# Attention followed by an expert layer on one core: biases from constants in two parts, v cast in halves, q on GpSimd, a mask bank taken at first need

## The chip, the cores and the metric

The kernel runs on one core of one Trainium2 chip. The metric is the device time of one execution in microseconds (us); lower is better. The *span*, from the first to the last instruction of the core in the profile's records, is given beside it. In each comparison the kernels ran on the same chip, interleaved with the kernel before. An execution is called slow when it is over 1.5% above the fastest of its kernel. A few executions at a clock of 0.989 to 0.992 stayed under the 1.5% and count as fast; two of them (224.36 and 225.21 us) are among the seven of the kernel before that e5 to e8 are compared with, and make the ratios of these four look better by about 0.2% (the mean of the seven is 223.54 us, that of the other five 223.04).

## The reference

```python
def reference(q, k, v, n_sink, window, moe_w_in, moe_w_out):   # cut
    scores = (q @ k.T) / sqrt(64)             # 4 batches, 8 heads, 768 tokens, head size 64
    keep = (pos_k < 4) | ((0 <= pos_q - pos_k) & (pos_q - pos_k < 128))
    a = softmax(where(keep, scores, -1e9))
    x = heads side by side of (a @ v)         # 3072 tokens x 512
    h = x @ moe_w_in                          # 512 x 2048
    return (h * sigmoid(1.702 * h)) @ moe_w_out   # 2048 x 512
```

## The kernel before

The work is cut into 12 blocks of 256 tokens. For each block, q, k and v are loaded as float32 and cast to float16. TensorE transposes q and k, multiplies them to scores, and ScalarE takes the exponential. TensorE then multiplies the probabilities by v, VectorE normalizes, and two matrix products (called expert matmuls here: first with w_in, then with w_out) follow. A planner in the kernel assigns every operation to an engine and a place in that engine's order. So a change in one duration or limit can reorder many instructions. The program fixes those orders; the chip then follows them with semaphores.

```python
# constants: identity and four 0/1 triangles, one load on GpSimd's queue
return np.concatenate([np.eye(P), rel <= 0, rel > 0, rel >= 0, rel < 0, sink], axis=1)
...
mask = bank[7][:, 0:448].bitcast(FP16)       # one PSUM bank of eight holds the keep-masks throughout
plan = Plan(7, {"s": 5, "t": 4, "a": 2, "x": 2, "h": RTH, "o": 2})   # seven banks for the rest
...
def with_sinks():                             # "seen", on GpSimd: what the masks are made from
    nc.gpsimd.tensor_copy(out=seen, in_=const[:, P : 3 * P])
    nc.gpsimd.memset(seen..., 1.0)
def masks():                                  # 7 transposes on TensorE into the mask bank
    ...
def biases(n, x, w, eng=nc.vector):           # 0/1 -> 0/-60000, on chip
    eng.tensor_scalar(out=bias[...], in0=const[...], scalar1=HIDE, scalar2=-HIDE, op0=ALU.mult, op1=ALU.add)
...
CAST_QK = ["DVE ACT", "POOL DVE"] + ["POOL"] * (NK - 2)               # engines by block
CAST_V = ["POOL DVE ACT", OPT.get("V1", "POOL DVE")] + ["POOL"] * (NK - 2)
...
LOADS = ["a0", "a1", "w0", "w1", "w2", "w3", "w4", "w5", "a2", "w6", "w7", "v2"]
# w0..w3: blocks of w_in, w4..w7: blocks of w_out, 512 KB landed each, all on GpSimd's queue
...
# expert matmuls with w_out, for j in 0, 1 (two token halves, 128 tokens each):
#   for s in 0..7: two matmuls, reading block w4 + s // 2 of w_out
deps = [o_g[k, s], o_w[4 + s // 2]] + ([prev] if prev else [])
...
# warm(_): matmuls of zeros that fill TensorE's empty time at the start
```

The softmax here doesn't subtract the row's maximum and nothing guards it: scores larger than these inputs give would overflow.

## Time and profile before

| | before |
|---|---|
| device time, median of 44 fast executions in the experiments' comparisons | 223.04 us |
| span, median of the same | 221.0 us (220.4 to 223.2) |
| TensorE busy | 97% of the span |
| TensorE empty between 7.58 and 20.77 us | 0.89 + 1.03 = 1.92 us |

TensorE is nearly full. So what a change of the opening can win lies in the first 21 us: the two stretches in which it stands empty, and the moment when the first real work starts. The view of what TensorE waits for, from 7 to 217 us of the kernel before, lists releaser, total us, number of waits, longest us:

```profile
PE bank L711 <- DVE xn L692: 0.9, 2, 0.6
PE bank L672 <- DVE blkT L281: 0.9, 1, 0.9
```

There are two kinds of wait and nothing else.

These are the timelines of VectorE (in a window so narrow that one cast stands alone) and of GpSimd around it. Columns: start, us, engine and line, operation, output and input, count, and idle time before it with what ended it.

```profile
6.86 0.66 DVE L281 CAST qk<-qk 128x512 f16<-128x512 f32 x1 [0.54 <-DMA qk<-in_q_dram]
```

```profile
5.97 0.93 POOL L318 TENSOR_SCALAR bias<-const 128x128 f16<-128x128 f16 x3
6.85 0.39 POOL L306 COPY seen<-const 128x256 f16<-128x256 f16 x1
7.30 0.27 POOL L307 MEMSET seen<- 128x8 f16 x1
```

The cast at 6.86 is that of the second half of q, and by the program's semaphores it is the one that the first transposes wait for. It ends at 7.52, and the transposes start at 7.58. In a wider window this cast is one of a group of three with 1.33 us together, 0.44 each.

### The profile page before, as it was taken

Reading aid. Unit: us, or ns where it says so; the run is one execution under the profiler, and the core shown is the slowest. Engines: PE = TensorE matmul, PEld = TensorE weight load, DVE = VectorE, ACT = ScalarE, POOL = GpSimd, SP = SyncE. Lnnn points to the kernel's source line nnn. Section 1 sums busy time; section 2 is a strip of 40 time slices with the busy share of each in tenths; the row PEclk is TensorE's granted clock in tenths of the full one; section 3 lists DMA queues with packets and bytes.
Section 4 is the critical chain, followed back from the end, with each engine's and each line's share of the span. In section 5 each row is a group of like instructions: output and inputs, shape, how many; then the busy total and the mean of one; then the engine's idle time right before and its main releaser. Section 6 shows DMA issues by size and latency. Waiting matters only on the chain.

```text
span 221.0 us, 5211 instructions
## 1 busy us (share of the span) xinstructions
PE 214.4 (97%) x2065; PEld 143.9 (65%) x2065; DVE 127.3 (58%) x278; ACT 125.1 (57%) x241; POOL 87.9 (40%) x151
## 2 busy tenths in 40 slices
PE   7979999999999999999999999999999999999993
PEld 2545977576756766766666667767667666666642
DVE  2796865388726765665555664675464655634310
ACT  3486544776647675566476475465476476444320
POOL 2795340848990865803905826607500000000000
PEclk9999999999999999999999999999999999999999
DMA  5999999999749779289399579399442212221223
GB/s 178 349 223 207 209 299 242 322 298 274 159 97 231 199 152 315 58 152 290 97 198 267 75 177 276 71 215 241 95 98 49 61 37 47 50 65 30 50 47 95
DMA packets 65767, 36.44 MB, mean 165 GB/s; under 512 B 27952, under 2 KB 60976, under 8 KB 65744
## 3 DMA queue, kind: packets, MB, share of 16 engines
q1 hardware_dynamic: 60704, 30.06, 54.9%
q0 software_dynamic: 4592, 5.41, 12.8%
q10 hardware_dynamic: 448, 0.66, 1.0%
q8 instruction: 16, 0.26, 0.5%
q14 instruction: 7, 0.06, 0.1%
HBM read 27.46 MB, written 6.29 MB: 153 GB/s over the span
## 4 chain that ended last, share of the span: by engine, by line
PE 90%; DMA 3%; DVE 3%; POOL 1%; issue 1%; ACT 0%; SPq 0%; POOLq 0%
PE bank L739 38%; PE bank L768 36%; PE bank L672 6%; PE bank L607 5%; DMA const<-const 2%; PE bank L536 2%; DVE v L281 1%; DMA out_dram<-osb 1%; DVE xn L692 1%; PE bank L588 1%; PE bank L600 1%; PE bank L711 1%; POOL bias L318 0%; DVE blkT L281 0%; ACT osb L787 0%
## 5 line engine op out<-in xcount | busy, mean ns | idle before, releaser
L768 PE MATMUL bank<-w_out,gT 128*128 128x512 f16 (+2 forms) x400 | 99.8, 371 | 0.0
L739 PE MATMUL bank<-xT,w_in 128*128 128x256 f16 x768 | 99.4, 273 | 0.0
L753 DVE SCALAR_TENSOR_TENSOR gT<-th,bank 128x512 f16<-128x512 f16 x96 | 65.5, 683 | 48.9 <-ACT th L751 48.0
L751 ACT ACTIVATE th<-bank 128x512 f16<-128x512 f32 x96 | 57.7, 603 | 62.4 <-PE bank L739 59.2
L739 PEld LDWEIGHTS <-w_in 128*128 128x128 f16 x768 | 73.1, 98 | 23.7 <-issue 1.6
L281 POOL CAST qk<-qk 64x512 f16<-64x512 f32 (+1 forms) x73 | 44.5, 612 | 44.1 <-DMA qk<-in_q_dram 35.3
L632 ACT ACTIVATE at<-bank 128x512 f16<-128x512 f32 (+1 forms) x96 | 48.9, 571 | 10.3 <-PE bank L607 10.0
L768 PEld LDWEIGHTS <-gT 128*128 128x128 f16 x400 | 36.0, 98 | 23.3 <-issue 1.4
L639 DVE TENSOR_TENSOR at<-at,bank 128x1024 f16<-128x1024 f16 (+1 forms) x40 | 25.7, 643 | 22.8 <-ACT at L632 22.8
L281 POOL CAST v<-v 64x512 f16<-64x512 f32 x42 | 25.9, 616 | 8.8 <-DMA v<-in_v_dram 6.8
L672 PE MATMUL bank<-v,at 128*128 128x65 f16 x352 | 21.0, 193 | 0.9 <-DVE blkT L281 0.9
L787 ACT ACTIVATE osb<-bank 128x512 f32<-128x512 f32 (+1 forms) x24 | 14.3, 594 | 12.1 <-PE bank L768 12.1
L672 PEld LDWEIGHTS <-at 128*128 128x128 f16 x352 | 17.5, 97 | 4.8 <-issue 1.0
L692 DVE TENSOR_TENSOR xb<-bank,rcp 128x256 f16<-128x256 f32 x36 | 15.2, 421 | 0.7
L672 PE MATMUL bank<-vs,ats 128*128 128x65 f16 x128 | 14.7, 193 | 0.0
L607 PEld LDWEIGHTS <-blkT 64*128 64x128 f16 x256 | 8.0, 94 | 8.7 <-issue 7.3
L607 PE MATMUL bank<-blkT 64*128 64x256 f16 x192 | 13.4, 244 | 0.0
L672 PEld LDWEIGHTS <-ats 128*128 128x128 f16 x128 | 11.9, 97 | 2.0 <-issue 0.2
L690 DVE RECIPROCAL rcp<-bank 128x4 f32<-128x4 f32 x48 | 8.4, 176 | 4.7 <-PE bank L672 4.2
L849 PE MATMUL bank<-zero 128*128 128x512 f16 x18 | 6.7, 545 | 1.2 <-DVE zero L295 1.2
L281 ACT COPY blkT<-bank 128x256 f16<-128x256 f16 (+1 forms) x13 | 5.3, 463 | 4.2 <-PE bank L536 4.2
L607 PE MATMUL bank<-blkT,blkT 64*128 64x128 f16 x64 | 7.2, 222 | 0.0
(46 smaller groups left out, 70.9 us busy)
## 6 DMA issues: line engine op xcount, KB each, us to landing
v<-in_v_dram SPq DMA_DIRECT2D x12, 512.0 KB, 6.7
out_dram<-osb SPq DMA_DIRECT2D x46, 128.0 KB, 2.5
qk<-in_q_dram SPq DMA_DIRECT2D x8, 512.0 KB, 4.7
qk<-in_k_dram SPq DMA_DIRECT2D x8, 512.0 KB, 6.1
w_in<-in_moe_w_in_dram POOLq DMA_DIRECT2D x4, 512.0 KB, 9.3
w_out<-in_moe_w_out_dram POOLq DMA_DIRECT2D x4, 512.0 KB, 12.9
qk<-in_q_dram SPq DMA_DIRECT2D x6, 256.0 KB, 5.2
qk<-in_k_dram SPq DMA_DIRECT2D x4, 256.0 KB, 5.2
```

What stands on the lines that cost most here:

```text
L281: {"POOL": nc.gpsimd.tensor_copy, "DVE": nc.vector.tensor_copy, "ACT": nc.scalar.copy}[e](out=out, in_=in_)
L607: nc.tensor.matmul(f32(o_s, 2 * n + i)[:, c : c + w], src[d, j], Q[d].rearrange("d j s -> d (j s)")[:, q0 : q0 + w], start=k >= KM, stop=T ...
L632: nc.scalar.activation(out=A[:, i, 0:W], in_=f32(o_s, 2 * n + i)[:, 0:W], func=AF.Exp, scale=scale)
L639: nc.vector.tensor_tensor(out=A[:, :, 0:W], in0=A[:, :, 0:W], in1=mask[:, c0 : c0 + W].unsqueeze(1).to_broadcast((P, 2, W)), op=ALU.mult,)
L672: nc.tensor.matmul(avp()[:, j, i], a_, v_, start=(n == 0), stop=(n == len(mms) - 1))
L690: o_r = op("DVE", 93, 190, lambda: nc.vector.reciprocal(out=rc, in_=avp()[:, :, :, D]), [o_a], prio=base - 1.2 * h8, kind="rcp")
L692: o_n = op("DVE", 340, 430, lambda: nc.vector.tensor_tensor(out=X, in0=avp()[:, :, :, 0:D], in1=rc.to_broadcast((P, 2, 2, D)), op=ALU.mult ...
L739: nc.tensor.matmul(f32(holder[0])[:, bass.ts(e, TB)], w_in16[:, c, bass.ts(Fi, P)], X[:, c] if k < KX else X2[:, :, c], start=(c == 0), st ...
L751: o_t = op("ACT", 477, 600, lambda first=first: nc.scalar.activation(out=th[first.places[0]], in_=f32(first), func=AF.Tanh, scale=0.851), ...
L753: o_g[k, s] = op("DVE", 590, 700, lambda first=first, s=s: nc.vector.scalar_tensor_tensor(out=g[:, 2 * s : 2 * s + 2].rearrange("p a t -> ...
L768: nc.tensor.matmul(f32(holder[0])[:, 0:w], g[:, Fi, bass.ts(j, P)], w_out16[:, Fi, c0:c1], start=(Fi == 0), stop=(Fi == NF - 1),)
L787: nc.scalar.mul(O[:, c0:c1], f32(holder[0])[:, 0:w], 0.5)
```

## The change

The intent is to clear the opening. The biases come ready-made from memory, the first v can be used when half of it is cast, and TensorE's masks and their PSUM bank are moved to where they are first needed. The planner also gets other numbers, which reorder the opening.

```diff
+    return [np.concatenate(x, axis=1).astype(np.float16) for x in (
+        [np.eye(P), low * sees, up * sees, low], [up, low, rel <= 0, rel > 0, sink])]
...
-        dma_free = {True: 0.0, False: 0.0}
+        dma_free = {True: 0.0, False: 2000.0}
...
-    mask = bank[7][:, 0:448].bitcast(FP16)
-    plan = Plan(7, {"s": 5, "t": 4, "a": 2, "x": 2, "h": RTH, "o": 2})
+    plan = Plan(8, {"m": 1, "s": 5, "t": 4, "a": 2, "x": 2, "h": RTH, "o": 2})
...
+    o_more = op("SP", 450, (350, 8), lambda: nc.sync.dma_start(more, const_d[1].ap()), prio=NEVER + 14.55, kind="loadv")
-    o_bias = [op("DVE", ..., first_biases, ...), op("POOL", ..., more_biases, ...)]
-    o_seen = op("POOL", 450, 550, with_sinks, [o_ident], prio=NEVER + 9, kind="const")
-    o_mask.begin = 7500.0
+    o_seen = op("POOL", 450, 550, with_sinks, [o_more], prio=NEVER + 1000, kind="const")
+    o_mask.begin = OPT.get("MB", 13000.0)
...
-    CAST_V = ["POOL DVE ACT", OPT.get("V1", "POOL DVE")] + ["POOL"] * (NK - 2)
+    CAST_V = ["POOL DVE ACT", OPT.get("V1", "POOL DVE ACT")] + ["POOL"] * (NK - 2)
...
-        return nominal(k - 1, slot - (... OPT.get("E1", 2) if k == 1 else 0))
+        return nominal(k - 1, slot - (... OPT.get("E1", 0) if k == 1 else 0))
...                                            # block 0: second half of k before that of q
-    prio=prio + (h / 2 + e / 8 if k == 0 ...)
+    prio=prio + (h / 2 + (1 - e) / 8 if k == 0 ...)
-                    o.late = 300.0
+                    o.late = OPT.get("Q0", 50.0)
...                                            # q of block 1: GpSimd
-    plan.any(cast(512, CAST_QK[k]), ...)
+    plan.any(cast(512, CAST_QK[k] if k != 1 else "DVE ACT" if e else OPT.get("Q1", "POOL")), ...)
...
+        parts = 2 if k == 0 else 1             # v of block 0 in two halves of the heads
...
-    order = plan.run(warm=warm, warm_until=12000.0, late_bank=12500.0)
+    order = plan.run(warm=warm, warm_until=OPT.get("WU", 9000.0), late_bank=OPT.get("WU", 9000.0) + 500.0)
```

More of the change, by code (lines that the diff above doesn't have):

```diff
@@ L24, in _token_of, with _build_constants @@
     return 2 * (kappa % 64) + kappa // 64
-def _build_constants() -> np.ndarray:
+HIDE = 60000.0
+def _build_constants() -> list:
     t = _token_of()
     rel = t[None, :] - t[:, None]
+    low, up = HIDE * (rel >= 0) - HIDE, HIDE * (rel < 0) - HIDE
+    sees = np.where(t[:, None] < 4, 0.0, 1.0)
     row = np.arange(P)
     sink = (row[:, None] // 16 == np.arange(8)[None, :]) & (row[:, None] % 16 < 4)
-    return np.concatenate([np.eye(P), rel <= 0, rel > 0, rel >= 0, rel < 0, sink], axis=1).astype(np.float16)
+    return [np.concatenate(x, axis=1).astype(np.float16) for x in (
+        [np.eye(P), low * sees, up * sees, low], [up, low, rel <= 0, rel > 0, sink])]
 class Op:
@@ L223 @@
     KT, KX, AHEAD = globals().get('OPT',{}).get('KT',4), 3, globals().get('OPT',{}).get('AHEAD',0)
-    RB, KM, HIDE = 4, globals().get('OPT',{}).get('KM',2), 60000.0
+    RB, KM = 4, globals().get('OPT',{}).get('KM',2)
     RS, RQ, RV, RA, RX, RG, RTH, RO = 3, 2, 4, 6, 3, 5, 3, 3
@@ L228 @@
     psp = ctx.enter_context(tc.tile_pool(name="ps", bufs=1, space=bass.MemoryType.PSUM))
-    const_d = nc.inline_tensor(_build_constants(), name="const16")
+    const_d = [nc.inline_tensor(x, name=f"const16_{n}") for n, x in enumerate(_build_constants())]
     def ring(name, n, shape, dt):
         return [pool.tile(list(shape), dt, name=f"{name}{i}") for i in range(n)]
-    const = pool.tile([P, 5 * P + H], FP16, name="const")
+    const = pool.tile([P, 4 * P], FP16, name="const")
+    more = pool.tile([P, 4 * P + H], FP16, name="more")
     ident = const[:, 0:P]
@@ L238 @@
     perm = pool.tile([P, P], FP16, name="perm")
-    bias = pool.tile([P, 7, P], FP16, name="bias")
     dummy = pool.tile([P, 8], FP16, name="dummy")
@@ L281, in copy, with mask @@
         {"POOL": nc.gpsimd.tensor_copy, "DVE": nc.vector.tensor_copy, "ACT": nc.scalar.copy}[e](out=out, in_=in_)
+    def mask(a, b):
+        return bank[o_mask.banks[0]][:, 0:448].bitcast(FP16)[:, a:b]
     users = {}
@@ L293 @@
     NEVER = -1e9
+    OPT = globals().get("OPT", {})
     VS_AT = NEVER + 14.505
     o_zero = op("DVE", 100, 200, lambda: nc.vector.memset(zero, 0.0), prio=NEVER, kind="const")
-    o_ident = op("POOL", 700, (300, 8), lambda: nc.gpsimd.dma_start(const, const_d.ap()), prio=NEVER - 1, kind="load")
-    o_ident.late = 1200.0
+    o_ident = op("POOL", 700, (450, 8), lambda: nc.gpsimd.dma_start(const, const_d[0].ap()), prio=NEVER - 1, kind="load")
+    o_ident.late = 900.0
+    o_more = op("SP", 450, (350, 8), lambda: nc.sync.dma_start(more, const_d[1].ap()), prio=NEVER + 14.55, kind="loadv")
     def ones():
@@ L304, in with_sinks @@
     def with_sinks():
-        nc.gpsimd.tensor_copy(out=seen, in_=const[:, P : 3 * P])
+        nc.gpsimd.tensor_copy(out=seen, in_=more[:, 2 * P : 4 * P])
         nc.gpsimd.memset(
@@ L311, in masks @@
     def masks():
-        low, up = const[:, P : 2 * P], const[:, 2 * P : 3 * P]
+        low, up = more[:, 2 * P : 3 * P], more[:, 3 * P : 4 * P]
         for n, x in enumerate((up, low, up, low, seen[:, 0:P], seen[:, P : 2 * P], low)):
-            nc.tensor.transpose(mask[:, bass.ts(n, P)], x, ident)
-    def biases(n, x, w, eng=nc.vector):
-        eng.tensor_scalar(
-            out=bias[:, n : n + w].rearrange("p n s -> p (n s)"), in0=const[:, (3 + x) * P : (3 + x + w) * P],
-            scalar1=HIDE, scalar2=-HIDE, op0=ALU.mult, op1=ALU.add,
-        )
-    def first_biases():
-        biases(0, 0, 2)
-        biases(2, 0, 1)
-        for t in range(2):
-            nc.vector.memset(bias[64 * t : 64 * t + n_sink // 2, 0:2], 0.0)
-    def more_biases():
-        biases(3, 1, 1, nc.gpsimd)
-        biases(4, 0, 2, nc.gpsimd)
-        biases(6, 0, 1, nc.gpsimd)
-    o_bias = [op("DVE", 550, 650, first_biases, [o_ident], prio=NEVER + 3, kind="const"),
-              op("POOL", 650, 750, more_biases, [o_ident], prio=NEVER + 8, kind="const")]
-    o_seen = op("POOL", 450, 550, with_sinks, [o_ident], prio=NEVER + 9, kind="const")
-    o_mask = op("PE", 7 * pe_ns(P), 7 * pe_ns(P) + 200, masks, [o_seen], prio=12000.0, kind="const")
-    o_mask.begin = 7500.0
+            nc.tensor.transpose(mask(n * P, n * P + P), x, ident)
+    o_seen = op("POOL", 450, 550, with_sinks, [o_more], prio=NEVER + 1000, kind="const")
+    o_mask = op("PE", 7 * pe_ns(P), 7 * pe_ns(P) + 200, masks, [o_seen], prio=12000.0, acq=("m", 1), kind="const")
+    o_mask.begin = OPT.get("MB", 13000.0)
     o_perm = op("POOL", 330, 450, lambda: nc.gpsimd.tensor_copy(
@@ L389, in attend @@
     def attend(k, slot):
-        return nominal(k - 1, slot - (AHEAD if k >= KX else OPT.get("E1", 2) if k == 1 else 0))
+        return nominal(k - 1, slot - (AHEAD if k >= KX else OPT.get("E1", 0) if k == 1 else 0))
     def slots(c16):
@@ L419, in f @@
                         )
-                    lq[e].append(op(eng, 780 if k == 2 else 450, (850 if k == 3 else 700, 8), f, war, prio=prio + (h / 2 + e / 8 if k == 0 else e / 2 + h / 8), kind="load"))
+                    lq[e].append(op(eng, 780 if k == 2 else 450, (850 if k == 3 else 700, 8), f, war, prio=prio + (h / 2 + (1 - e) / 8 if k == 0 else e / 2 + h / 8), kind="load"))
             else:
@@ L459, in f @@
                              dst[:, e].rearrange("s h i d -> s (h i d)").rearrange("s (h a i d) -> s h a i d", h=2, a=4, i=2)[:, h])
-                    o_cqk[k, e, h] = plan.any(cast(512, CAST_QK[k]), f, [lq[e][h]] + war,
+                    o_cqk[k, e, h] = plan.any(cast(512, CAST_QK[k] if k != 1 else "DVE ACT" if e else OPT.get("Q1", "POOL")), f, [lq[e][h]] + war,
                                               prio=nominal(k - 1, -7 + 2 * h) if k else NEVER + h, kind="cqk")
@@ L465, in load @@
         war = reuse("v16", k % RV)
-        w = H // len(o_lv)
-        for n, o_l in enumerate(o_lv):
+        parts = 2 if k == 0 else 1
+        w = H // parts
+        for n in range(parts):
+            o_l = o_lv[0]
             got = []
@@ L474, in f @@
                         copy(eng, w16[64 * i : 64 * i + 64, j, h, 0:D], dv[64 * j : 64 * j + 64, h, i])
-                    o = plan.any(cast(D * w, CAST_V[k]), f, [o_l] + war + [o_ones],
+                    ns = cast(D * w, CAST_V[k])
+                    if k < 2 and "DVE" in ns:
+                        ns["DVE"] = (60 * w + 70, 60 * w + 170)
+                    o = plan.any(ns, f, [o_l] + war + [o_ones],
                                  prio=(nominal(k - 1, -4) if k else NEVER + 5 + n), kind="cv")
@@ L484, in f @@
                     out=vs16[:, b].rearrange("r p i e -> r (p i) e"), in0=vs32[:, b].unsqueeze(1).to_broadcast((P, H, E)),
-                    in1=const[:, 5 * P : 5 * P + H].unsqueeze(2).to_broadcast((P, H, E)), op=ALU.mult,
+                    in1=more[:, 4 * P : 4 * P + H].unsqueeze(2).to_broadcast((P, H, E)), op=ALU.mult,
                 )
-            o_vs[b] = op("POOL", 1100, 1200, f, [*o_vl, o_ident], prio=nominal(k - 1, 0) if k else load_at("w2") + 5, kind="vs")
+            o_vs[b] = op("POOL", 1100, 1200, f, [*o_vl, o_more], prio=nominal(k - 1, 0) if k else load_at("w2") + 5, kind="vs")
             o_vs[b].begin = max(0.0, nominal(k - 2, 0))
@@ L600, in s @@
                         nc.tensor.matmul(
-                            f32(o_s, 2 * n + i)[:, 0:W], ident, bias[:, 3:7] if r else bias[:, 0:3], start=True, stop=False,
+                            f32(o_s, 2 * n + i)[:, 0:W], ident,
+                            more[:, 0 : 2 * P].unsqueeze(1).to_broadcast((P, 2, 2 * P)) if r else const[:, P : 4 * P], start=True, stop=False,
                             skip_group_check=True,
@@ L613, in scores @@
         if k < KM:
-            deps = deps + [o_bias[1 if r else 0]]
+            deps = deps + [o_more if r else o_ident]
         dur = len(pairs) * (W / 2.4 + 5) * (3 if k < KM else 1) + 190 + (120 if sinks else 0)
@@ L640, in m @@
                     out=A[:, :, 0:W], in0=A[:, :, 0:W],
-                    in1=mask[:, c0 : c0 + W].unsqueeze(1).to_broadcast((P, 2, W)), op=ALU.mult,
+                    in1=mask(c0, c0 + W).unsqueeze(1).to_broadcast((P, 2, W)), op=ALU.mult,
                 )
@@ L819 @@
     mm2(NK - 1)
-    loads += o_vl
+    loads += o_vl + [o_more]
     loads.sort(key=lambda o: (o.prio, o.seq))
@@ L844 @@
         gates.append((o, g))
-    warm_bank = bank[6]
+    warm_bank = bank[7]
     def warm(_):
```

## The prediction

> **What bounds the kernel now.** I began with the page: engine totals, then the row of TensorE.
>
> ```profile
> PE 214.4 (97%) x2065; PEld 143.9 (65%) x2065; DVE 127.3 (58%) x278; ACT 125.1 (57%) x241; POOL 87.9 (40%) x151
> ...
> PE   7979999999999999999999999999999999999993
> ```
>
> TensorE (PE) is the bound, and its row has holes only in the first four slices (22 us) and in the last one. The change touches only the opening, so what it can win is TensorE time wasted there. The view by stage, cut where TensorE's work changes, sizes it:
>
> ```profile
> 0.00:7.58 7.58, 6.33 (x17) 1.00 0.67 237
> 7.58:13.74 6.16, 5.27 (x64) 1.00 1.15 287
> 13.74:20.77 7.03, 6.00 (x93) 1.00 1.24 206
> 20.77:37.21 16.44, 16.44 (x174) 1.00 1.17 237
> 37.21:200.00 162.79, 162.79 (x1607) 1.00 0.67 163
> ```
>
> Columns: stage, its length, TensorE busy time with instructions, granted clock, DMA share, GB/s. Up to 7.58 the 17 matmuls only warm the array. To 20.77, 0.89 + 1.03 = 1.92 us are empty. After 20.77 there is no hole to 200. Idle to be won is thus under 2 us of 223.3, plus what the first transposes can be moved forward. TensorE's timeline names the holes:
>
> ```profile
> 7.58 1.07 PE L536 MATMUL bank<-perm,qk 128*128 128x128 f16 x16
> ...
> 8.88 0.38 PE L849 MATMUL bank<-zero 128*128 128x512 f16 x1
> ...
> 12.52 0.34 PE L607 MATMUL bank<-blkT 64*128 64x256 f16 x4
> 13.74 0.53 PE L672 MATMUL bank<-v,at 128*128 128x65 f16 x12 [0.88 <-DVE blkT L281]
> ...
> 16.01 0.29 PE L711 MATMUL bank<-const,xn 128*128 128x128 f16 x2 [0.59 <-DVE xn L692]
> ...
> 20.77 1.04 PE L739 MATMUL bank<-xT,w_in 128*128 128x256 f16 x8
> ```
>
> The hole at 13.74 is the first probabilities-times-v waiting for VectorE (DVE), which still empties the PSUM bank that it will write. The hole at 16.01 is VectorE's normalization. The wait view of TensorE alone, 7 to 217 us, lists only these: 0.9 us in two waits for xn, 0.9 us in one for blkT.
>
> Then I asked what may come next once these holes close, and looked at the weights. They arrive on the GpSimd queue (q0), one behind the other; the last block of w_out is issued at 24.15. Below: its issue in the GpSimd timeline, its row in the DMA view of 23 to 38 us, and TensorE around its first use.
>
> ```profile
> 24.15 0.76 POOL L376 DMA_DIRECT2D w_out<-in_moe_w_out_dram  x1 [1.75 <-DMA w_in<-in_moe_w_in_dram]
> ...
> w_out<-in_moe_w_out_dram POOLq DMA_DIRECT2D x1, 512.0 KB, 12.9
> ...
> 36.78 0.60 PE L739 MATMUL bank<-xT,w_in 128*128 128x256 f16 x4
> 37.21 1.03 PE L768 MATMUL bank<-w_out,gT 128*128 128x512 f16 x4
> ```
>
> It lands at 24.15 + 12.9 = 37.05 us. The four matmuls at 37.21 are the first that read it: in the program's order of TensorE they are the fourth group of w_out matmuls of the first token block, chunks 12 to 15. So TensorE gets there 0.16 us after the data. This is no wait in the profile, and yet it is a second limit, right behind the first.
>
> **What the Trainium skill says.** (1) "DMA: Bandwidth & Descriptors", SWDGE vs HWDGE vs iDMA: a cast during DMA is only possible from GpSimd, and only one software queue is allocated. The trace agrees: all eight weight blocks (float32 in memory, float16 in SBUF) and block 2's q and k share q0. (2) The same page, Queues, rings and completion order: each DMA engine takes turns between its queues packet by packet. The trace agrees. The DMA view gives for 14 to 15 us (q0 alone), for 12.3 to 13.1 us (both) and for 10 to 12.3 us (q1 alone):
>
> ```profile
> q0 software_dynamic: 207, 0.21, 125.3%
> ...
> q0 software_dynamic: 88, 0.09, 69.3%
> q1 hardware_dynamic: 240, 0.12, 52.3%
> ...
> q1 hardware_dynamic: 1256, 0.59, 116.4%
> ```
>
> Alone q0 moves 207 packets in 1 us; with q1 beside it 88 in 0.8 us, 110 per us. (3) "Perfetto Trace Analysis", DMA Instruction — SWDGE (GPSIMD): the profiled end of such an issue is the end of descriptor generation, not of the movement. Here: 0.76 us of issue, 12.9 us to landing. So issuing w_out earlier would not help; it stands in a queue.
>
> **The change part by part.** Durations are those of the timelines before.
>
> *Biases from constants.* This drops two tensor-scalars (0.43 us) and two memsets (0.39 us) from VectorE at 5.53 to 6.32, and three from GpSimd (0.93 us). VectorE then waited 0.54 us, to 6.86, for the last half of q: the removed 0.82 us lies beside that wait and wins nothing by itself. On GpSimd the freed time takes both q casts of block 1 (0.61 us each), which come after landings at about 7.6 and 8.2; it is done by about 8.9, so the first weight issue (9.18, held by a k landing at 8.9) doesn't move.
>
> *First transposes.* All four q/k casts of block 0 go to VectorE, k first. q still lands at 6.86, cast to 7.29. In the new order 16 warming matmuls stand ahead of them, not 17: the last ones take about 0.25 us, so they end at about 7.3. The transposes start some 0.25 us sooner. The seven mask transposes (0.39 us) leave this place but three warming matmuls (about 0.65 us) stand in it instead of one (0.22), so first scores start 0.2 to 0.3 us sooner.
>
> *Eighth bank and v in halves.* The first two probabilities-times-v now write banks emptied long before, so the 0.88 us hole no longer depends on the three blkT copies. What is left is v: landed at 11.7 (its first VectorE cast starts at 11.72), eight half casts over three engines, first half ready at about 12.4. Scores and transposes end at 12.86 - 0.2, so the start is near 12.7: a further 0.8 us.
>
> *Second v.* VectorE from 11.69 to 19.67 (last xT copy) is busy 7.19 of 7.98 us. It loses two of three casts of block 1's v (0.62, 0.74, 0.44: about 1.2 us) and 0.3 us on block 0's v, and gets one blkT copy more (0.36): net -1.1 us. ScalarE (ACT) gets two casts of 0.62 us, but waited 1.27 us at 17.42.
>
> The masks come later (0.39 us, just moved). Together: TensorE begins the expert matmuls at about 19.0 to 19.6 instead of 20.77, about 1.2 us won.
>
> *What takes it back.* From there to the first use of the last weight block, TensorE's order holds the same work in both programs, except that the last piece of block 1's attention now stands behind the start: adding up durations gives 17.3 us against 16.6. So TensorE would arrive at 19.3 + 17.2 = 36.5 us, before the landing. Counted from the very start, work up to that use differs by only about 0.2 us, and the remaining work behind it is equal. And the landing gets no earlier: the first weight issue stays at 9.18, q0's bytes are the same. It gets a little later: the second constant part is 128 x 520 x 2 bytes = 0.133 MB on q1 ahead of v of block 1. q1 alone moves 0.59 MB in 2.3 us, so it needs 0.5 us; beside q0 (0.12 MB in 0.8 us) 0.9 us. While both run q0 loses 97 of 207 packets, 47%: 0.24 to 0.42 us later. The first constant part is 34 KB smaller, at 257 GB/s about 0.1 us earlier for everything behind it. Net: +0.2 us. TensorE stalls at about 36.5, resumes at about 37.4, and ends 0.2 us later than now. **Sum: 223.31 + 0.2 = 223.5 us.**
>
> **Rivals.** *A, the whole head start survives*: 223.3 - 1.2 = 222.1 us. It would need the weights to land a microsecond earlier; for it speaks only that TensorE shows no wait for w_out before. Against it: 0.16 us between landing and use. *B, my choice*: the landing of the last w_out block holds TensorE: 223.5. *C, the late v*: the extra load also makes v of block 1 wait for a later landing before it is issued (about 0.6 us later), and ScalarE has its casts ahead of block 1's exponentials. If v lands at 14.7 instead of 13.86, up to 1 us of the head start is lost; but B leaves about 0.9 us of slack, so C costs at most some tenths: 223.3 to 224. *D, GpSimd late with weights*: its v cast now waits in front of the fourth weight issue (14.47, then about 15). q0 still has two blocks queued then, so no gap: no effect.
>
> **Range and chances.** The three runs before lie within 0.17 us. B has about 0.7 of my belief, a partial A 0.2, C beyond the slack 0.1. Both limits are within 1.3 us of today's time, 2% would be 4.5 us; nothing in the opening is that large. I predict 223.5 us, range 222.6 to 224.3; faster by over 2%: 0.01, within 2%: 0.98, slower: 0.01.
>
> **What would show it.** Right: no hole before the first probabilities-times-v near 12.7 to 13; expert matmuls from about 19 to 19.6; a new TensorE wait for w_out of 0.5 to 1.2 us near 36.5; first use of that block at about 37.4; equal length from there. Wrong: that wait missing with an earlier end (A: the last block landed early), or expert matmuls starting after 20 us (C), or holes after 38 us, where I expect none.

## The result

Before: 223.34 us median of 4 executions. Changed: 221.89 us median of 4, of which three are fast (221.81, 221.57, 221.97) and one is slow (227.01, clock 0.985). The ratio of the fast executions is 0.9931, 95% interval 0.9912 to 0.9951. A ratio here is the mean time of one kernel's fast executions over that of the other's of the same rounds, so not quite the ratio of the medians quoted. The change is faster, by about 0.7%, which counts as "within 2%". The prediction had the class right, but its range of 222.6 to 224.3 missed the time.

Over all comparisons, seven fast executions of the changed kernel have medians of 221.84 us and a span of 220.1, against 223.04 and 221.0 before. So 0.9 us of the gain of 1.2 lies in the span. The rest is time outside it, 2.0 us for the kernel before and 1.8 us for the changed one. That part goes with no part of the change: e2 below is the kernel before with one more transfer and has 1.8 us too. I therefore compare spans from here on where tenths matter.

The view by stage of the changed kernel, cut at the same places of the work as in the prediction (first transposes, first probabilities times v, first expert matmul, fourth group of w_out matmuls). Columns: stage, its length, then busy time with instructions of TensorE, its weight loads, VectorE, ScalarE and GpSimd, granted clock, DMA share and GB/s.

```profile
0.00:6.88 6.88, 4.94 (x17) 1.82 (x17) 2.15 (x10) 1.49 (x2) 1.76 (x7) 1.00 0.63 205
6.88:12.43 5.55, 5.50 (x60) 3.05 (x61) 3.95 (x10) 4.51 (x13) 4.18 (x8) 1.00 1.11 328
12.43:18.88 6.45, 5.60 (x94) 3.37 (x92) 5.29 (x20) 6.38 (x15) 6.18 (x12) 1.00 1.23 216
18.88:36.23 17.35, 17.35 (x183) 14.02 (x180) 12.99 (x27) 9.96 (x18) 5.95 (x9) 1.00 1.20 235
```

The stages now give a ledger up to the fourth w_out group, which starts at 36.23 and not at 37.21. The first transposes start 0.70 us earlier (7.58 to 6.88). Empty time behind them is 0.05 + 0.85 = 0.90 and was 1.92, so 1.02 less. Busy time behind them is 5.50 + 5.60 + 17.35 = 28.45 and was 5.27 + 6.00 + 16.44 = 27.71, so 0.74 more, of which 0.43 are two more warming matmuls. The sum is 0.70 + 1.02 - 0.74 = 0.98 us ahead. The expert matmuls begin 1.89 us earlier, but 0.91 of that (17.35 - 16.44) is a piece of block 1's attention that now stands behind their start. The ledger shows where the time went in these two executions; it doesn't show which edit moved it.

TensorE's timeline after, at the points that the prediction named:

```profile
6.88 1.29 PE L532 MATMUL bank<-perm,qk 128*128 128x128 f16 x16 [0.74 <-DVE qk L286]
8.00 0.81 PE L846 MATMUL bank<-zero 128*128 128x512 f16 x3
...
12.43 0.69 PE L669 MATMUL bank<-v,at 128*128 128x65 f16 x12
...
14.06 0.38 PE L596 MATMUL bank<-more,const 128*128 128x512 f16 x1 [0.73 <-ACT at L629]
...
18.88 1.03 PE L736 MATMUL bank<-xT,w_in 128*128 128x256 f16 x8
...
35.79 0.60 PE L736 MATMUL bank<-xT,w_in 128*128 128x256 f16 x4
36.23 1.03 PE L765 MATMUL bank<-w_out,gT 128*128 128x512 f16 x4
```

The hole before the first probabilities times v is gone. A new one of 0.73 us stands at 14.06, where ScalarE's exponential has not yet freed a bank. And the wait at 36.23, on which the prediction rested, is not there. TensorE's waits from 7 to 217 us are these two and no other:

```profile
PE bank L532 <- DVE qk L286: 0.7, 1, 0.7
PE bank L596 <- ACT at L629: 0.7, 1, 0.7
```

The last matmul starts at 217.29 us before and at 216.32 after: 0.97 us ahead. So the head start of 0.98 us was kept to the end.

### Which weights are read when

The view of TensorE's w_out groups of the kernel before shows why no wait could appear:

```profile
29.80 1.03 PE L768 MATMUL bank<-w_out,gT 128*128 128x512 f16 x4
...
31.54 1.03 PE L768 MATMUL bank<-w_out,gT 128*128 128x512 f16 x4
...
35.91 1.03 PE L768 MATMUL bank<-w_out,gT 128*128 128x512 f16 x4
...
38.51 1.89 PE L768 MATMUL bank<-w_out,gT 128*128 128x512 f16 x8
```

Between 35.91 and 38.51 lies the group at 37.21 that the prediction shows. I had counted four groups as the four weight blocks in a row. The semaphores on the instructions say otherwise. The groups at 29.80 and 31.54 wait for blocks w4 and w5. The group at 35.91 waits for no load: it is the *second* token half, which reads w4 again. The group at 37.21 waits for w6, which landed at 34.56. The last block, w7, landed at 37.09 and is first waited for by the second four of the eight at 38.51, about 39.38. So the slack was 37.21 - 34.56 = 2.65 us on w6 and 39.38 - 37.09 = 2.3 us on w7, and not 0.16.

In the changed kernel w6 landed at 35.30 and is read at 36.23; w7 landed at 37.88 and is first read at 37.53 + 6 x 0.215 = 38.82 (its order has two more matmuls of older blocks first). The slack is 0.93 and 0.94 us. The landings moved back by 0.74 to 0.79 us and the reads forward by 0.98 or less, so in this execution more than half of the slack is used up, but nothing waits. Landings differ between executions: in the profile of e1_again, the same kernel, w6 landed at 34.67 and was read at 36.28, w7 at 37.24 and 38.87, which leaves 1.6 us each.

### The profile page after: what moved, and what is told of

Read it like the earlier page. It is cut to its first block, busy times and chain, and to the rows that moved or that the text cites. A ratio compares the mean times of both kernels' runs of the same rounds, so it can differ in the third digit from the quotient of the medians.

```text
span 220.0 us, 5209 instructions
## 1 busy us (share of the span) xinstructions
PE 213.7 (97%) x2066; PEld 143.8 (65%) x2066; DVE 125.9 (57%) x274; ACT 125.7 (57%) x243; POOL 87.0 (40%) x150
## 4 chain that ended last, share of the span: by engine, by line
PE 91%; DMA 4%; ACT 2%; SPq 1%; issue 0%; DVE 0%
PE bank L736 39%; PE bank L765 37%; PE bank L669 6%; PE bank L604 5%; DMA qk<-in_q_dram 3%; PE bank L532 1%; DMA out_dram<-osb 1%; ACT at L629 1%; ACT v L286 1%; PE bank L596 1%; PE bank L584 1%; PE bank L708 1%; SPq L407 0%; PE bank L846 0%; ACT blkT L286 0%
## 5 line engine op out<-in xcount | busy, mean ns | idle before, releaser
L286 POOL CAST v<-v 64x512 f16<-64x512 f32 (+1 forms) x43 | 26.1, 606 | 8.9 <-DMA v<-in_v_dram 6.8
L846 PE MATMUL bank<-zero 128*128 128x512 f16 x19 | 5.8, 463 | 1.2 <-DVE zero L304 1.2
```

Of the source, the lines that this page charges most:

```text
L286: {"POOL": nc.gpsimd.tensor_copy, "DVE": nc.vector.tensor_copy, "ACT": nc.scalar.copy}[e](out=out, in_=in_)
```

## The experiments

"Alone" means that a part is put into the kernel before, "undone" that it is taken out of the changed kernel. All gave a correct result. Spans and times are medians of fast executions.

| label | what | fast runs | us | span | ratio to before, 95% interval |
|---|---|---|---|---|---|
| e1_again | changed kernel again | 4 | 221.88 | 220.1 | 0.9935 (0.9899 to 0.9972) |
| e2_late_w_before | before + 512 KB ahead of w6 | 6 | 223.32 | 221.5 | 1.0003 (0.9973 to 1.0033) |
| e3_late_w_half | changed + 256 KB ahead of w6 | 4 | 222.66 | 220.75 | 0.9965 (0.992 to 1.0009) |
| e4_late_w_full | changed + 512 KB ahead of w6 | 5 | 222.81 | 220.9 | 0.9981 (0.9948 to 1.0015) |
| e5_undo_bank | changed, eighth bank undone | 3 | 222.49 | 220.5 | 0.9952 (0.9893 to 1.001) |
| e6_undo_v_act | changed, ScalarE's v of block 1 undone | 4 | 221.59 | 219.6 | 0.9905 (0.9856 to 0.9954) |
| e7_bank_alone | bank and later masks alone | 3 | 222.36 | 220.4 | 0.996 (0.9881 to 1.0038) |
| e8_v_act_alone | ScalarE's v of block 1 alone | 4 | 222.57 | 220.55 | 0.9952 (0.9903 to 1.0001) |
| e9_bias_work_back | changed + the bias work, unused | 3 | 221.79 | 219.8 | 0.9952 (0.9925 to 0.9979) |
| e10_v_whole | changed, halves undone | 3 | 221.31 | 219.5 | 0.9926 (0.9906 to 0.9946) |
| e11_q_shared | changed, q on GpSimd undone | 4 | 222.01 | 219.85 | 0.9956 (0.9936 to 0.9976) |
| e12_ident_first | e6 + identity loaded alone first | 3 | 221.64 | 219.9 | 0.9935 (0.9911 to 0.9958) |
| e13_v_both | e6 and e10 together | 5 | 221.59 | 219.6 | 0.9965 (0.9923 to 1.0006) |
| e14_v_act_undone_again | e6 again | 4 | 221.69 | 219.7 | 0.9952 (0.9928 to 0.9977) |
| e15_undo_bank_v_act | e5 and e6 together | 4 | 222.26 | 220.1 | 0.9972 (0.9955 to 0.9989) |
| e16_plan_alone | the load plan alone | 4 | 223.11 | 221.1 | 1.0005 (0.9988 to 1.0022) |
| e17_masks_late | later masks alone, seven banks | 6 | 222.43 | 220.6 | 0.9981 (0.9954 to 1.0008) |
| e18_plan_all | all of the order, none of the data changes | 6 | 222.14 | 220.1 | 0.9963 (0.9939 to 0.9987) |

Apart from the result, the changed kernel itself ran beside e2 to e4 only, as e1, on another chip than e5 to e18. Where these are set against its 220.1 us below, the bridge is the kernel before, which ran in every comparison. The fast executions of before in these five comparisons had median spans of 221.0, 221.1, 221.1, 221.0 and 221.1. One execution of before in the comparison of e9 to e12 took 1240 us; it is an outlier without an explanation and is left out.

### Were the weights the second limit? (e1 to e4)

**e1_again** is the changed kernel itself, to have more of its executions.

> The changed kernel once more, as the yardstick of this call. If the gain is the 1.0 us by which TensorE ran ahead in its trace, the time is 221.6 to 222.3 us and the expert matmuls start at about 18.9 us again, with no TensorE wait for w_out; if the start of the transposes (6.88 us) was luck of that one execution, they start nearer to 7.3 and the gain is smaller.

Measured: 221.88 us, span 220.1. The result stands. Two more executions were slow (225.01 and 228.08).

The other three put one more transfer into GpSimd's queue ahead of w6, which delays w6 and w7:

```diff
+            if j == 6:
+                extra = pool.tile([P, 4, 512], FP16, name="extra")      # e3: 2 and src[:, 0:2]
+                nc.gpsimd.dma_start(extra, src[:, 0:4])
             return nc.gpsimd.dma_start(to, src)
```

**e2_late_w_before**, in the kernel before:

> The kernel before, with one more 512 KB transfer in the GpSimd queue ahead of the last two w_out blocks, so that these land some 2.5 us later (at 205 GB/s). My prediction's reading (block lands at 37.05 us, first used at 37.21, slack 0.16) says: about 2.3 us slower. The rival, from the order of the instructions: the matmuls at 37.21 read the last block but one (landed 34.56), and the last block (37.09) is first read near 39.37, slack 2.3 us or more for both: at most 0.3 us slower.

**e3_late_w_half** and **e4_late_w_full**, in the changed kernel:

> The changed kernel with a further 256 KB transfer ahead of the last two w_out blocks: they land 1.25 us later. Slack theory (in the changed kernel the last two blocks land 0.93 us before use): a new TensorE wait of about 0.3 us, time up by about 0.3 us against the changed kernel. If the landing already held TensorE: up by 1.25 us. If weights don't matter at all: no change.

> The same with 512 KB: they land 2.5 us later. Slack theory: TensorE waits about 1.6 us for w_out, time up by about 1.6 us. If the landing already held TensorE: 2.5 us. If weights don't matter: no change.

In e2 the last block landed at 39.60 us, 2.5 later than before. These are TensorE's waits in e2:

```profile
PE bank L717 <- DVE xn L698: 0.9, 2, 0.6
PE bank L678 <- DVE blkT L281: 0.9, 1, 0.9
PE bank L542 <- POOL seen L307: 0.3, 1, 0.3
PE bank L774 <- DMA w_out<-in_moe_w_out_dram: 0.2, 1, 0.2
```

A delay of 2.5 us makes a wait of 0.2 us, so the slack was about 2.3 us. With a slack of 0.16 us the wait would have been about 2.3. The span grew by 0.5 us, and the time hardly (ratio 1.0003). That refutes the prediction's limit in one line.

In e4 the wait that I had predicted for the changed kernel does appear, but only once the weights are made late on purpose. Its waits, and the group that reads w6:

```profile
PE bank L771 <- DMA w_out<-in_moe_w_out_dram: 0.9, 1, 0.9
PE bank L602 <- ACT at L635: 0.8, 1, 0.8
```

```profile
36.99 1.02 PE L771 MATMUL bank<-w_out,gT 128*128 128x512 f16 x4 [0.92 <-DMA w_out<-in_moe_w_out_dram]
```

Here w6 landed at 36.95, 1.65 us later than in the changed kernel, and cost 0.92 us of wait. The span grew by 0.8 us. The expectation was 1.6 us and missed: it took the slack from the other profile. In e4 the extra transfer landed at 34.41, which is about where w6 would have landed without it, and TensorE would have been there at 36.07, so the slack is estimated at 1.66 us. So the changed kernel stands 0.9 to 1.7 us from this limit, by execution, and one more transfer of that size reaches it.

e3 says nothing on the weights: w6 landed at 36.19 and was read at 37.49, so the wait of 0.3 us that was expected isn't there. In its profiled execution TensorE was late for another reason:

```profile
PE bank L675 <- ACT at L635: 1.1, 1, 1.1
PE bank L602 <- ACT at L635: 0.9, 1, 0.9
```

Block 1's v landed at 15.94 us there, and at 14.06 in the changed kernel's profile. ScalarE has the casts of this v in its order ahead of the exponentials:

```profile
15.96 1.25 ACT L286 CAST v<-v 64x512 f16<-64x512 f32 x2 [0.96 <-DMA v<-in_v_dram]
17.12 1.55 ACT L635 ACTIVATE at<-bank 128x512 f16<-128x512 f32 x3
```

The exponentials begin at 17.12, against 15.85 in the changed kernel, and the expert matmuls at 20.14 against 18.88: both 1.26 to 1.27 us later. This is rival C of the prediction, here at its full size.

### The bank and ScalarE's v (e5 to e8, e14, e15)

**e5_undo_bank**:

```diff
-    plan = Plan(8, {"m": 1, ...})
+    plan = Plan(7, {"m": 1, ...})            # masks fixed in bank[7], warming matmuls in bank[6]
```

> The changed kernel with PSUM bank 7 kept for the mask from the start, seven banks for everything else, as before. If the eighth bank closed the hole ahead of the first probabilities-times-v (0.88 us before), a hole of some 0.5 to 0.9 us is back there or soon after and the time goes up by about 0.7 us. Rival: v's landing (11.7 us) and the casts hold that place anyway, and the bank is worth under 0.2 us.

**e6_undo_v_act**:

```diff
-    OPT.get("V1", "POOL DVE ACT")
+    OPT.get("V1", "POOL DVE")
```

> The changed kernel with the casts of block 1's v shared by GpSimd and VectorE alone, as before, none on ScalarE. If VectorE's chain in the stretch of 12 to 19 us sets the start of the expert matmuls, up to 1.2 us of casts come back onto it and the time goes up by 0.5 to 1.0 us. Rival: ScalarE is the bound there now (TensorE's one hole of 0.73 us in the changed kernel waits for its exponentials), and taking two casts of 0.62 us from it pays for what VectorE gets: under 0.3 us.

**e7_bank_alone** puts the eighth bank and the later masks into the kernel before; **e8_v_act_alone** lets ScalarE cast block 1's v there ("POOL DVE" to "POOL DVE ACT").

> The kernel before with the eighth bank alone (mask bank taken at first need, masks later). Holes theory: the 0.88 us wait for blkT goes, the waits for xn stay; 0.3 to 0.7 us faster than before. Rival (v's landing and casts hold that place): no change.

> The kernel before with ScalarE admitted to the casts of block 1's v and nothing else; the order on TensorE is unchanged. If VectorE's chain is the bound in 14 to 19 us, the 0.9 us of waits for xn shrink and the time falls by 0.5 to 0.9 us. Rival: ScalarE's exponentials take over at once, under 0.3 us.

e5 is 0.4 us of span slower than the changed kernel, so the bank is worth about that. It is not what closed the hole before the first probabilities times v, for without it that hole is gone, too. The wait behind it grows from 0.73 to 1.11 us, and one of 0.42 stands at 16.50:

```profile
12.44 0.53 PE L669 MATMUL bank<-v,at 128*128 128x65 f16 x12
14.07 0.59 PE L596 MATMUL bank<-more,const 128*128 128x512 f16 x2 [1.11 <-ACT at L629]
```

e7 doesn't isolate the bank: it also moves the masks, which alone give 220.6 (e17 below), and in its profile 0.91 us of waits for v and blkT stand before and among the first probabilities times v. e6 is 0.5 us *faster*, which neither side of its expectation foresaw, so giving v of block 1 to ScalarE costs. Yet alone, in e8, the same edit seems to win 0.5 us (its ratio interval just reaches 1). The busy times from 12 to 19 us fit the two signs. One line each for before, e8, e6 and the changed kernel; the columns are those of the view by stage:

```profile
12.00:19.00 7.00, 5.15 (x69) 2.46 (x66) 6.62 (x19) 5.16 (x13) 6.33 (x10) 1.00 1.23 214
```

```profile
12.00:19.00 7.00, 5.22 (x70) 2.55 (x67) 5.63 (x17) 6.37 (x15) 6.45 (x10) 1.00 1.22 210
```

```profile
12.00:19.00 7.00, 6.21 (x97) 3.52 (x95) 6.13 (x21) 6.27 (x15) 6.37 (x11) 1.00 1.23 219
```

```profile
12.00:19.00 7.00, 6.15 (x103) 3.88 (x101) 5.78 (x21) 6.91 (x16) 6.73 (x13) 1.00 1.23 221
```

Before, VectorE is the fuller of the two (6.62 of 7.00) and ScalarE has 1.84 us free; moving v to ScalarE evens them out. In the changed kernel the opening is denser, TensorE does 6.15 us of work there and not 5.15, and with v ScalarE is busy 6.91 of 7.00 us. In e6 VectorE has 6.13 and ScalarE 6.27: neither is full. ScalarE's timelines agree: in e6 the exponentials that follow the second blkT copy begin at 13.95 and run on, while in the changed kernel only one runs before the casts of 14.70, and the next begin at 15.85.

The wait at 14.06 is not the price of these casts: it ends before they begin, and e6 has it, too (0.79 us, to 13.86). The price stands one step later. In e1_again ScalarE waits for v to land, casts it, and TensorE waits for an exponential behind it:

```profile
14.75 1.25 ACT L286 CAST v<-v 64x512 f16<-64x512 f32 x2 [0.38 <-DMA v<-in_v_dram]
15.91 1.54 ACT L629 ACTIVATE at<-bank 128x512 f16<-128x512 f32 x3
```

```profile
16.55 0.35 PE L669 MATMUL bank<-v,at 128*128 128x65 f16 x6 [0.47 <-ACT at L629]
```

All seven fast profiles of the changed kernel and its variants with these casts on ScalarE have a hole there: 0.12 us in four (changed kernel, e4, e9, e11), 0.42 in e5, 0.47 in e1_again, 1.06 in e3. None of e6, e13 and e15, with the casts taken off ScalarE, has one, and the only one of e12 after 15 us waits for VectorE. So this hole is shown to go with the casts; it covers a part of the 0.5 us, and more in some executions than in others.

**e14_v_act_undone_again** repeats e6, and **e15_undo_bank_v_act** takes both edits out.

> e6 once more, as yardstick of this call and to see whether it beats the changed kernel again: spans of 219.3 to 219.6 us against 219.8 to 220.2. If e6 was luck, its spans are those of the changed kernel.

> The changed kernel with neither the eighth bank nor ScalarE for block 1's v. Without the bank (e5) about 0.45 us of the gain was left, spans 220.5 to 220.7 against 221.0. If that rest came from ScalarE's share of v (which alone won 0.4 us in the kernel before, e8), it is gone here: spans of about 221.0. If it came from the earlier front (order of the first casts, no bias work, masks later), it stays: 220.2 to 220.6.

e14 gives 219.7 (219.4, 219.6, 219.8 and one of 221.0): e6 holds. (Its profile and that of e10 fell in slow executions and are not read.) e15 gives 220.1. So of the distance from 221.0 to the changed kernel's 220.1, the bank gives about 0.5 (e15 to e6), ScalarE's v takes 0.5 back, and 0.9 remains that is neither.

### Which part carries the remaining 0.9 us? (e9 to e13, e16 to e18)

**e9_bias_work_back** puts the bias arithmetic back on VectorE and GpSimd, into a tile that nothing reads:

```diff
+    op("DVE", 550, 650, first_biases, [o_ident], prio=NEVER + 3, kind="const")
+    op("POOL", 650, 750, more_biases, [o_ident], prio=NEVER + 8, kind="const")
```

> The changed kernel with the removed instructions put back as work without use (VectorE: two tensor-scalars and two memsets, 0.82 us; GpSimd: three tensor-scalars, 0.93 us); the order on TensorE is unchanged. My step (the removed 0.82 us lies beside VectorE's wait for the last half of q): no change, under 0.2 us, and the first transposes start no later than in the changed kernel. Rival (VectorE's first casts are the path): the transposes start about 0.5 us later and the time goes up by 0.3 us or more, because k of block 0 is cast by VectorE now, too.

**e10_v_whole** (`parts = 1`) and **e11_q_shared** (`cast(512, CAST_QK[k])` for all blocks):

> The changed kernel with block 0's v cast in whole pieces again; the order on TensorE is unchanged. If the halves let the first probabilities-times-v start sooner (12.1 to 12.4 us against a landing of v at 11.4 to 11.7), that start moves back by 0.3 to 0.6 us; whether it reaches the end depends on the wait for ScalarE just behind it (0.7 to 0.9 us), which then only gets shorter: time up by 0 to 0.3 us.

> The changed kernel with block 1's q cast by GpSimd or VectorE as the planner likes, as before; the order on TensorE is unchanged. My step says that this part only uses time that GpSimd has: no change, under 0.2 us. Rival: VectorE's cast delays its copies of block 0's transposes (7.5 us) and with them the first scores: up by about 0.3 us.

**e12_ident_first** takes e6 and loads the identity alone first, the first biases on ScalarE's queue; **e13_v_both** takes e6 and e10 together:

> An attempt to beat both: the kernel of e6 (v of block 1 not on ScalarE) with only the identity (32 KB) in the first constant load, and the first biases (96 KB) on ScalarE's queue behind the two k loads. If the landings of k and q set the first transposes, 96 KB less ahead of them is worth some 0.1 to 0.25 us: 0.1 to 0.3 us faster than e6. Rival: the halves land as they did (they start within 0.3 us of each other from run to run anyway), no change.

> The changed kernel with both v parts of the change undone: block 0's v cast whole, block 1's v not on ScalarE. e6 won 0.4 us over the changed kernel by the second, e10's fast runs some 0.3 us by the first. If both free ScalarE ahead of the exponentials that TensorE waits for, they add up in part: spans of about 219.0 to 219.4 us, the best of the study. Rival: VectorE's casts of v then set the pace: no better than e6 (219.3 to 219.6).

**e16_plan_alone** puts three edits of the load plan into the kernel before (`dma_free` 2000, second half of k first, `late` 50):

> The kernel before with only the planner's three assumptions of the change (transfers 2 us later, k of block 0 ahead of q, 50 ns instead of 300 for the later halves). They move block 0's four casts to VectorE and reorder TensorE's front. If the rest of the gain comes from this order, spans fall from 221.0 to about 220.5. Rival: the bias instructions that are still there (0.82 us on VectorE) and the masks in the front keep it at 221.0.

None of these carries the gain. e9 is not slower than the changed kernel (219.8), so the removed bias work was worth nothing. e10 is 0.6 us faster, where 0 to 0.3 us slower was expected, so the halves bring nothing and probably cost a little. e11 has 219.85: q on GpSimd brings nothing. e12 has no gain over e6. e16 is at 221.1, like before. e13 is a miss: 219.6 like e6, with outliers to 222.5.

What was left is order: when the masks are made and where block 1's attention stands. **e17_masks_late**:

```diff
-    o_seen = op("POOL", 450, 550, with_sinks, [o_ident], prio=NEVER + 9, kind="const")
+    o_seen = op("POOL", 450, 550, with_sinks, [o_ident], prio=NEVER + 1000, kind="const")
+    o_seen.begin = 10000.0
-    o_mask.begin = 7500.0
+    o_mask.begin = 13000.0
```

> The kernel before with one thing moved: GpSimd makes the keep-masks' source (seen) only after 10 us and TensorE transposes the masks (7 transposes, 0.4 us) at their first need, not between the first transposes and the first scores. Bank count, loads, biases and casts as before. In four profiles of the kernel before's family the first transposes start 0.27 to 0.29 us after the cast that their semaphore waits for (second half of q), while in six profiles of the changed family without GpSimd work beside that cast the lag is 0.05 to 0.06 us. Theory 'GpSimd beside the cast costs the 0.2 us': lag falls to about 0.06, first transposes 0.2 us earlier relative to the landing of q, first biases 0.5 to 0.6 us earlier (the masks are gone from there too), and the span falls to about 220.5 from 221.0. Rival 'the lag is the cast's own': lag stays 0.28, first biases 0.4 us earlier. Rival 'what is won at the front is eaten by the wait for blkT before the first probabilities times v': span stays at 220.9 to 221.2 whatever the front does.

**e18_plan_all** adds to e17 the load plan of e16, block 1's attention two slots later (`E1` 0) and warming planned to 9 us:

> The kernel before with all of the change's ordering and none of its data changes: masks late as in e17, block 1's attention placed two slots later, warming matmuls planned to 9 us rather than 12, and the load order of e16 (second half of k before that of q, so the first transposes wait for k). Seven banks, biases computed on chip, v of block 0 whole, no v on ScalarE in block 1. If the 0.9 us that e15 keeps over the kernel before is order alone: span about 220.1, expert matmuls from 19.6 to 19.9, their start beside that of e15 (19.69). If it needs the constants in two parts, the halves or q on GpSimd: span 220.6 to 221.1. In executions where the first load on the SP queue (q) lands before the one on ScalarE's queue (k), as in the profile of e16, the first transposes should come about 0.6 us later than in the others, near 7.3 to 7.5 against 6.8.

e17 has a span of 220.6 (five of six between 220.5 and 220.7), 0.5 below before; the interval of its ratio still contains 1. e18 has 220.1, and its interval excludes 1. This is the span of e15. **The order of the work alone carries the remaining 0.9 us**, without constants in two parts, without halves, without q on GpSimd; about half of it is the masks' move. The other half is not split between the later block 1, the load plan and the warming. The trace of e18 shows what it got: the two waits for xn, 0.9 us together in before, are gone (0.28 us is left in e17), the first transposes come 0.35 us earlier, and two more warming matmuls take 0.43 of it.

The cast that the transposes wait for, and TensorE's timeline, in e17:

```profile
6.69 0.43 DVE L281 CAST qk<-qk 128x512 f16<-128x512 f32 x1 [0.56 <-DMA qk<-in_q_dram]
```

```profile
7.19 1.06 PE L537 MATMUL bank<-perm,qk 128*128 128x128 f16 x16
...
8.51 0.49 PE L601 MATMUL bank<-bias,const 128*128 128x384 f16 x2
```

What I had put as a lag behind a cast of 0.43 us is in the cast itself. Where GpSimd makes `seen` beside it the cast lasts 0.64 to 0.66 us (before, e2, e8, e16). Beside GpSimd's bias work it lasts 0.57 (e7, e9). With GpSimd idle, as in e17 and in the changed kernel, it lasts 0.43. The Trainium skill, "SBUF — State Buffer", section "Who interferes with whom", says that a VectorE cast in a two-port mode and a GpSimd instruction exclude each other. The measurement fits in direction: moving `seen` and the masks is the only edit of e17, and the cast is 0.23 us shorter. No view shows in which mode this cast runs. From first transposes to first biases it is 1.32 us in e17 and 1.52 before, as the masks no longer stand between.

### The order in which q and k land

One more thing came out of the profiles. The first load on ScalarE's queue (k) and the first on SyncE's (q) are issued within 0.01 us of each other, and which lands first differs by execution. In 17 of the 20 profiles k is ahead (4.36 against 5.04 in before); in e7, e16 and e18 q is (in e18 4.08 against 4.80). The second halves follow in the same order. The program, however, fixes which half the transposes wait for: by the semaphores the second half of q in the kernel before, of k in the changed one. Between the two profiles that is the main reason for the earlier start. The wait ended with the landing at 6.84 before and with that at 6.37 after, 0.47 of the 0.70 us; the other 0.23 are the cast, 0.66 us beside GpSimd before and 0.43 after. Where q wins the race it is the reverse: e18's transposes started at 7.23, its k having landed at 6.64. And e7's early first transposes (7.10) are owed to that race, so e7's profile says nothing on the bank. The swap of q and k alone doesn't reach the end: e16 has it, without the later masks, and its span is that of before.

The cast is not the only thing that can hold the first transposes. The program puts 16 warming matmuls before them (17 in before), and in each execution these step from 0.43 to 0.22 us at another time: at 4.02 in the changed kernel's profile, at 6.28 in before. In four of the eleven fast profiles of the changed kernel and its variants (e1_again, e3, e5, e11) the transposes begin 0.50 to 0.83 us after the cast's end, right behind the last warming matmul. In e1_again the step came at 5.73, the cast ended at 6.20, and the transposes began at 6.81; with the step at 6.28 the 16 would have lasted to about 7.15 (an estimate from before's timeline). So the start at 6.88, set by the cast, also needed a step before about 5.8.

## Why the prediction was wrong

*TensorE is the bound, and the winnable time is in the opening*: right. No hole appeared after 21 us in the changed kernel.

*Bias work beside waits wins nothing*: right for the end time (e9). At the front it stretched one cast from 0.43 to 0.57 us, which did not reach the end.

*First transposes some 0.25 us sooner, as 16 warming matmuls stand ahead and not 17*: wrong in cause and size. They came 0.70 us sooner. In before's profile they waited for the cast of q's second half, with GpSimd's copy beside it, and the last warming matmul ended at 7.53, just before the 7.58. I had the cast end at 7.29, with the mean of a group of three (0.44 us); the single cast lasts 0.66 and ends at 7.52. 

*Eighth bank and v in halves, probabilities times v near 12.7, the hole gone*: right in the result (12.43), not in the reason. Without the bank the hole is gone as well (12.44 in e5). With v whole 0.24 and 0.31 us of it come back (e13, at 12.51 and 13.07), but there the later wait of 0.73 us is missing, so the halves only moved the hole. The prediction had no wait for an exponential behind it. The bank is worth 0.4 to 0.5 us of span (e5, and e15 to e6); the halves nothing (e10).

*ScalarE takes two casts, as it waited 1.27 us at 17.42*: wrong. A wait in the old order is no room in the new one: the changed opening filled ScalarE to 6.91 of 7.00 us, the exponentials stand behind the casts, and the casts cost 0.5 us (e6).

*Expert matmuls from 19.0 to 19.6*: 18.88, a little early.

*Work up to the w_out group differs by only about 0.2 us*: it differs by 0.74 in busy time. I had not counted the two more warming matmuls (0.43), which look like work and are empty time.

*The landing gets later by 0.2 us*: right, as far as two profiles tell. In the changed kernel's profile it is 0.74 to 0.79 us, but this execution's loads were 0.2 to 0.3 late from the first on (k at 4.66 against 4.36); in e1_again it is 0.10 for w6 and 0.16 for w7.

*The last w_out block is first read at 37.21, 0.16 us after it landed, so it takes the head start back*: **this is the step that failed and made the number wrong.** Its words were "The four matmuls at 37.21 are the first that read it". They read the third block. The slack was 2.3 to 2.65 us (semaphores, landings, e2). Without this step my own sum was rival A, 222.1 us, and the measurement is 221.89. That agreement is in part luck: the start came 0.70 us sooner and not 0.25, a hole of 0.73 us was not foreseen, and the prediction's two sums for the head start (1.2 us, and 37.21 - 36.5 = 0.7) did not agree with each other; it measured 0.98. Rival A asked for weights that land earlier; it did not need that. The mechanism itself is real, as e4 shows, and is now 0.9 to 1.7 us away.

*Rival C, the late v*: real where v lands late: TensorE's hole behind ScalarE's casts is 1.06 us in e3 (v at 15.94) and 0.47 in e1_again (14.73). In the changed kernel's profile (14.06) ScalarE was busy until 14.67 anyway, and the hole is 0.12. *Rival D*: no wait of the kind is in any profile.

What stays open: why the time outside the span differs by 0.2 us between kernels; why block 1's v lands between 13.7 and 15.9 us in the fast profiles of the changed kernel and its variants, but between 13.3 and 14.0 where the load of the second constants is not ahead of it; and whether the lower clock has to do with the kernel: it was under 0.995 in 14 of 62 executions of the changed kernel and its variants, and in 10 of 78 of the kernel before and its variants. The kernel with ScalarE's v undone (e6 and e14) was the best repeated one by median span, about 0.5 us under the changed kernel. By ratio it is not: 0.9905 in e6, whose before had two executions at a lower clock, and 0.9952 in e14, against 0.9931 and 0.9935. The intervals overlap, so a better version is likely and not proven.

## What to carry to other kernels

Before calling a landing the next limit, look up which instruction first waits for it in the program's semaphores; counting groups in a timeline can mix two loops that interleave. Idle time of an engine in the old order is no reserve for the new one: move work only where that engine's busy share in the *new* stage leaves room. And when many edits come together, try the reordering alone: here it gave 0.9 us, and the constants in two parts, the halves and q on GpSimd, which seemed the point, gave nothing that these runs can show.

## What the Trainium skill lacked or had wrong

- "TensorE: Matmul & The Clock Gate", section "What you observe", gives the change to the full rate at about 4 us into sustained matmuls, within 0.5 us. In the 20 profiles of these kernels, all of which begin their warming matmuls at 1.19 us, the step from 0.43 to 0.22 us per matmul came 2.8 us (changed kernel, at 4.02) to 5.8 us (e3, at 7.00) after that start. That is a spread of 3.0 us and not of 1. The next section of the page, "What's actually happening", does say that the number of slow matmuls varies from run to run, so only this figure is at odds. In e3 the late step held the first transposes until 7.44, although their cast had ended at 6.61.
- "SBUF — State Buffer", section "Who interferes with whom", says that the loser of the shared port blocks fully, and gives no cost for a cast beside GpSimd's small copies. In the kernel before the cast is recorded from 6.86 to 7.52 and GpSimd's copy from 6.85 to 7.24: they overlap, and the cast is 0.23 us longer, less than the copy's 0.39. Recorded times of GpSimd may be rough, so this does not refute the page.
- No page gives how often, and by how much, the first loads of two hardware queues, issued within 0.01 us, change their order of landing: here k was first in 17 profiles, q in 3, about 0.7 us apart.
- "DMA: Bandwidth & Descriptors", section "Queues, rings and completion order", says how two queues share an engine. It gives no spread of a landing: block 1's v took from 13.7 to 15.9 us in fast executions of almost the same program.
